# Attention with a gated feed-forward layer: projections as a stream of row-tile pairs, one-chunk score visits, AV of two head pairs a visit

## The chip, the cores and the metric

The kernel runs on one core of a Trainium2 chip. A span that the profile gives is a little shorter than the time (466.3 us beside 468.95 for the kernel before); spans are compared with spans and times with times.

## The reference

```
scores = q @ k.T / sqrt(64)                 # 8 batches, 12 heads, 448 positions, head size 64
attn   = max(scores, 0)**2 / 448
x      = (attn @ v), heads side by side     # 3584 x 768
xn     = x / sqrt(mean(x*x) + 1e-6) * rms_g
out    = (silu(xn @ w_gate) * (xn @ w_val)) @ w_out    # 768 -> 1536 -> 768
```

## The kernel before

Everything is bf16 into fp32 sums. Batch 0's attention runs first. Then, for each batch, the feed-forward layer of batch b (24 projections of 6 matmul steps, then 3 or 4 row blocks of the output projection of 12 steps) is the main stream on TensorE, and short visits of batch b+1's attention are woven into it, so that ScalarE and VectorE can work on relus and squares meanwhile.

A matmul that fills the array is issued as two **column tiles**: all 128 contraction rows, 64 output columns each (128x64). The two run side by side in one bank of PSUM:

```python
def project(b, *groups):                          # one or more of the 24 projections
    pss = [ps_m.tile([P, S], FP32, name="psP", tag="mm") for _ in groups]
    for kt in range(KT):
        for ps, (w_sb, fb) in zip(pss, groups):
            for h in range(0, P, D):              # two column halves
                nc.tensor.matmul(
                    out=ps[h : h + D, :], lhsT=w_sb[:, kt, fb * P + h : fb * P + h + D],
                    rhs=xns[b][:, kt, :], start=(kt == 0), stop=(kt == KT - 1))
```

The scores contract over 64 only, so they are **row tiles** (64x128): head 0 on rows 0 to 63, head 1 on rows 64 to 127, in two banks. A visit computes two chunks of keys; every second visit is followed by AV of the head pair before:

```python
for j in range(HP):                               # 6 head pairs
    add(0.5, lambda j=j: scores(b, j, (0, 1)))    # two chunks a visit
    ...
    add(1.2, lambda j=j: scores(b, j, (2, 3)), lambda j=j: j and attend(b, j - 1))
```

PSUM has eight banks: two score buffers of two banks (`ps_s`), one for AV (`ps_a`), and three single banks (`ps_m`) for everything else. Gates (`psP<-xn,wg_sb`) are read by a silu on ScalarE, values (`psP<-xn,wv_sb`) by the product `hT` on VectorE, outputs (`psO`) by a copy on ScalarE. Relus are on ScalarE for three chunks of four and on VectorE for the fourth; squares are on VectorE.

Of the kernel before, what the change touches and what calls it, by code (L numbers as in the profile page):

```python
# [15 lines left out]


def merge(main, side, head=0.0, tail=0.0):


    total = sum(c for c, _ in main)
    if not main:
        return [f for _, f in side]
    out, done, k = [], 0.0, 0
    n = len(side)
    for c, f in main:
        while k < n and done >= total * (head + (1.0 - head - tail) * k / n):
            out.append(side[k][1])
            k += 1
        out.append(f)  # L30
        done += c
    out.extend(f for _, f in side[k:])
    return out
# [3 lines left out]
def kernel(  # L37
# [30 lines left out]
    apool = ctx.enter_context(tc.tile_pool(name="attn", bufs=10))  # L68
# [6 lines left out]
    ps_a = ctx.enter_context(tc.tile_pool(name="ps_a", bufs=1, space=bass.MemoryType.PSUM))  # L75
    ps_m = ctx.enter_context(tc.tile_pool(name="ps_m", bufs=3, space=bass.MemoryType.PSUM))
# [117 lines left out]
    def scores(b, j, cs):  # L194

        pss = []
        for c in cs:
            psS = ps_s.tile([P, 2, 512], FP32, name="psS", tag="psS")
            for hh in range(2):
                prt = slice(hh * D, (hh + 1) * D)  # L200
                nc.tensor.matmul(  # L201
                    out=psS[:, hh, :S],
                    lhsT=qkT[b][prt, j].rearrange("p t s -> p (t s)")[:, c * PC : c * PC + P],
                    rhs=qkT[b][prt, j, 1, :],
                    start=True,
                    stop=True,
                )
            pss.append(psS)
        squares = []
        for c, psS in zip(cs, pss):  # L210
            r = apool.tile([PC, 2, S], BF16, name="r", tag="r")
            if relu_on(b, j, c) == "dve":
                nc.vector.tensor_relu(out=r[:], in_=psS[:PC, :, :S])  # L213
            else:
                nc.scalar.activation(out=r[:], in_=psS[:PC, :, :S], func=ACT.Relu)  # L215
            eng = nc.gpsimd if square_on(b, j, c) == "pool" else nc.vector
            squares.append(
                lambda r=r, eng=eng: eng.tensor_tensor(out=r[:], in0=r[:], in1=r[:], op=ALU.mult)  # L218
            )
            rsq[b, j, c] = r  # L220
        flush()
        pending.extend(squares)
# [3 lines left out]
    def attend(b, j):  # L226
        psAV = ps_a.tile([P, S], FP32, name="psAV", tag="ps_a")
        for c in range(NCH):
            for hh in range(2):
                nc.tensor.matmul(  # L230
                    out=psAV[hh * D : (hh + 1) * D, :],
                    lhsT=ld["v", b][:, 2 * j + hh, c * D : (c + 1) * D],
                    rhs=rsq[b, j, c][:, hh, :],
                    start=(c == 0),
                    stop=(c == NCH - 1),
                )
        if j == 0:
            xTs[b] = xpool.tile([P, KT, S], BF16, name="xT", tag="xT")
            x2s[b] = npool.tile([P, KT, S], BF16, name="x2", tag="x2", bufs=1)
        xT = xTs[b]  # L240
        nc.scalar.mul(out=xT[:, j, :], in_=psAV[:], mul=inv_attn)  # L241
        pending.append(
            lambda: nc.vector.tensor_tensor(  # L243
                out=x2s[b][:, j, :], in0=xT[:, j, :], in1=xT[:, j, :], op=ALU.mult
            )
        )
# [74 lines left out]
    def gate(b, fb):  # L321
        silu(b, fb, *project(b, (wg_sb, fb)))
# [100 lines left out]
```

## Time and profile before

| | before |
|---|---|
| time, median of 3 | 468.95 us (468.29 to 469.0) |
| span of the profile | 466.3 us |
| TensorE busy | 97% |
| first gate matmul begins (batch 0's attention is over) | 38.6 us |

From the page of the kernel before: the engines' busy time with its share of the span, and what the chain that ended last consists of.

```profile
PE 454.5 (97%) x4768; PEld 257.6 (55%) x4768; DVE 283.6 (61%) x449; ACT 252.5 (54%) x380; POOL 55.8 (12%) x48
...
PE 91%; DVE 3%; ACT 2%; DMA 1%; issue 1%; POOL 0%; ACTq 0%; DVEq 0%; POOLq 0%
```

TensorE is the limit. The chain in order of time (start, duration, what) shows how near the stream is to its best, and where it is not. One cycle in the middle, and the last batch, which has no visits:

```profile
215.97 0.48 PE psS L201 x4
216.45 2.39 PE psP L302 x24
218.84 0.48 PE psS L201 x4
219.32 0.88 PE psAV L230 x8
220.20 2.27 PE psP L302 x24
...
418.56 27.24 PE psP L302 x288
445.80 15.62 PE psO L339 x192
```

The last two lines give the rates of an undisturbed stream: 27.24 us for 144 pairs is 189 ns for a 448-wide pair, and 15.62 us for 48 pairs each of 512 and 256 columns is 325 ns for the two together. A visit of two score pairs is 0.48 us where two such pairs are 0.38, and a further part of each mode change hides in the lines after it: the whole cycle takes 6.51 us for 32 pairs, which are 6.06 us.

The waits of TensorE on other engines, in us in total, times, and the longest:

```profile
PE psS L201 <- ACT r L215: 2.6, 7, 0.4
...
PE psAV L230 <- DVE r L218: 1.0, 4, 0.5
...
PE psP L302 <- ACT sil L312: 0.3, 1, 0.3
```

The last line is a projection of batch 0 that waits for its bank, right after three that end together. No other projection and no output waits for one. A caution on reading: the profile's end of a matmul is modelled (about 0.35 us for a 448-wide one, although the next may begin after 0.19), so an "idle before" of TensorE is shorter than the time lost. The Trainium skill says of that end, too, that it is an estimate ("Perfetto Trace Analysis", Summary: the profiler window per engine type: TensorE runs to an *estimated* end). For sums I therefore use starts alone: on one half of the array, from one matmul's start to the next one's start, less the spacing of an undisturbed stream (189 ns at 448 columns; 109 at 256 and 216 at 512, which make the 325). What is left over I call a **gap**, and sort it by what the later matmul waits for in the built program. Before, gaps after 38.6 us are 21.6 us, of which 16.3 stand at changes of tiling mode.

### The profile page before, as it was taken

The numbers are of one execution on the slowest core, as the hardware profiler recorded it, in microseconds if no ns is written. First come the engines' busy times: TensorE is split into PE (matmuls) and PEld (weight loads), VectorE is DVE, ScalarE is ACT, GpSimd is POOL, SyncE is SP. The second block draws the span as 40 slices with busy tenths as digits, with TensorE's granted clock in tenths as the row PEclk, the third lists the DMA queues.
The fourth block names the chain that finished last, engine by engine and source line by source line (L and its number), as shares of the span: only waits on it lengthen the run. The fifth ranks groups of instructions, "written<-read, shape, count | busy, mean of one in ns | idle before, by whom it ended". The sixth has DMA issues, their size and how long they took to land.

```text
span 466.3 us, 10899 instructions
## 1 busy us (share of the span) xinstructions
PE 454.5 (97%) x4768; PEld 257.6 (55%) x4768; DVE 283.6 (61%) x449; ACT 252.5 (54%) x380; POOL 55.8 (12%) x48
## 2 busy tenths in 40 slices
PE   7989999999999999999999999999999999999995
PEld 3336654655456445655456554565456554577774
DVE  2876497757745677557665578457773677562210
ACT  4872476566545666546645666546665566452221
POOL 8463000421012000400004000000000000000000
PEclk9999999999999999999999999999999999999999
DMA  9999999999919920499009940086001300021013
GB/s 113 200 204 200 209 168 129 116 208 158 82 33 173 201 29 1 53 214 135 1 2 143 211 83 1 7 173 103 1 2 38 100 2 1 0 70 34 1 37 101
DMA packets 128047, 43.56 MB, mean 93 GB/s; under 512 B 100608, under 2 KB 124416, under 8 KB 128000
## 3 DMA queue, kind: packets, MB, share of 16 engines
q0 software_dynamic: 88944, 23.60, 52.0%
q1 hardware_dynamic: 39056, 19.28, 20.9%
q8 instruction: 37, 0.61, 0.5%
q14 instruction: 10, 0.08, 0.1%
HBM read 47.19 MB, written 11.01 MB: 125 GB/s over the span
## 4 chain that ended last, share of the span: by engine, by line
PE 91%; DVE 3%; ACT 2%; DMA 1%; issue 1%; POOL 0%; ACTq 0%; DVEq 0%; POOLq 0%
PE psP L302 48%; PE psO L339 23%; PE psS L201 9%; PE psAV L230 8%; DVE r L218 2%; PE psB L139 1%; PE psSS L276 1%; DMA kb<-in_k_dram 1%; ACT r L215 1%; DVE r L213 1%; PE psT L174 1%; ACT xT L241 1%; DVE x L243 0%; POOL qb L93 0%; POOL kb L93 0%
## 5 line engine op out<-in xcount | busy, mean ns | idle before, releaser
L215 ACT ACTIVATE r<-psS 112x896 bf16<-112x896 f32 x147 | 128.4, 915 | 28.6 <-PE psS L201 28.4
L302 PE MATMUL psP<-xn,wv_sb 128*64 128x448 bf16 x1152 | 126.9, 353 | 0.3 <-ACT sil L312 0.3
L302 PE MATMUL psP<-xn,wg_sb 128*64 128x448 bf16 x1152 | 126.8, 353 | 0.0
L339 PE MATMUL psO<-wo_sb,hT 128*64 128x512 bf16 (+1 forms) x1344 | 112.5, 326 | 0.0
L317 DVE TENSOR_TENSOR hT<-sil,psP 128x448 bf16<-128x448 bf16 x96 | 59.6, 621 | 84.7 <-PE psP L302 82.6
L218 DVE TENSOR_TENSOR r<-r 112x896 bf16<-112x896 bf16 x189 | 109.9, 626 | 0.2 <-ACT r L215 0.2
L312 ACT ACTIVATE sil<-psP 128x448 bf16<-128x448 f32 x96 | 52.2, 545 | 97.2 <-PE psP L302 97.1
L339 PEld LDWEIGHTS <-hT 128*64 128x64 bf16 x1344 | 78.9, 110 | 31.7 <-issue 0.4
L302 PEld LDWEIGHTS <-wg_sb 128*64 128x64 bf16 x1152 | 66.4, 110 | 45.4 <-issue 7.4
L302 PEld LDWEIGHTS <-wv_sb 128*64 128x64 bf16 x1152 | 65.5, 110 | 46.7 <-issue 10.5
L346 ACT COPY ost<-psO 128x512 f32<-128x512 f32 (+1 forms) x56 | 26.7, 478 | 73.1 <-PE psO L339 73.1
L213 DVE TENSOR_SCALAR r<-psS 112x896 bf16<-112x896 f32 x45 | 49.0, 1089 | 27.6 <-PE psS L201 27.6
L201 PE MATMUL psS<-qkT 64*128 64x448 bf16 x384 | 54.0, 354 | 3.3 <-ACT r L215 2.6
L230 PE MATMUL psAV<-r,vb 112*64 112x448 bf16 x384 | 46.1, 358 | 1.0 <-DVE r L218 1.0
L285 DVE RECIPROCAL rstd<-rstd 128x448 f32<-128x448 f32 x8 | 23.6, 2953 | 19.9 <-ACT rstd L281 19.9
L201 PEld LDWEIGHTS <-qkT 64*128 64x128 bf16 x384 | 11.9, 94 | 37.7 <-issue 33.1
L230 PEld LDWEIGHTS <-vb 112*64 112x64 bf16 x384 | 18.4, 109 | 24.0 <-issue 15.3
L243 DVE TENSOR_TENSOR x<-xT 128x448 bf16<-128x448 bf16 x48 | 18.5, 385 | 20.7 <-ACT xT L241 20.7
L241 ACT ACTIVATE xT<-psAV 128x448 bf16<-128x448 f32 x48 | 26.2, 545 | 8.2 <-PE psAV L230 6.6
L93 POOL DMA_DIRECT2D vb<-in_v_dram x9 | 8.7, 970 | 178.7 <-PE psAV L230 177.5
L288 DVE SCALAR_TENSOR_TENSOR xn<-xT,g_sb,rstd 128x448 bf16<-128x448 bf16 x48 | 29.3, 680 | 0.3
L95 POOL DMA_DIRECT2D qb<-in_q_dram x6 | 13.8, 2299 | 43.7 <-DMA qkT<-qb 38.1
(29 smaller groups left out, 126.3 us busy)
## 6 DMA issues: line engine op xcount, KB each, us to landing
qb<-in_q_dram POOLq DMA_DIRECT2D x7, 672.0 KB, 13.4
kb<-in_k_dram POOLq DMA_DIRECT2D x7, 672.0 KB, 19.9
vb<-in_v_dram POOLq DMA_DIRECT2D x7, 672.0 KB, 8.2
out_dram<-ost SPq DMA_DIRECT2D x8, 336.0 KB, 3.7
wg_sb<-in_moe_w_gate_dram POOLq DMA_DIRECT2D x4, 576.0 KB, 18.0
wv_sb<-in_moe_w_val_dram POOLq DMA_DIRECT2D x4, 576.0 KB, 19.7
wo_sb<-in_moe_w_out_dram POOLq DMA_DIRECT2D x2, 1152.0 KB, 26.2
out_dram<-ost SPq DMA_DIRECT2D x8, 288.0 KB, 4.6
```

Source lines behind the costliest of these rows:

```text
L201: nc.tensor.matmul(out=psS[:, hh, :S], lhsT=qkT[b][prt, j].rearrange("p t s -> p (t s)")[:, c * PC : c * PC + P], rhs=qkT[b][prt, j, 1, :] ...
L213: nc.vector.tensor_relu(out=r[:], in_=psS[:PC, :, :S])
L215: nc.scalar.activation(out=r[:], in_=psS[:PC, :, :S], func=ACT.Relu)
L218: lambda r=r, eng=eng: eng.tensor_tensor(out=r[:], in0=r[:], in1=r[:], op=ALU.mult)
L230: nc.tensor.matmul(out=psAV[hh * D : (hh + 1) * D, :], lhsT=ld["v", b][:, 2 * j + hh, c * D : (c + 1) * D], rhs=rsq[b, j, c][:, hh, :], st ...
L241: nc.scalar.mul(out=xT[:, j, :], in_=psAV[:], mul=inv_attn)
L288: nc.vector.scalar_tensor_tensor(out=xn[:, kt, :], in0=xTs[b][:, kt, :], scalar=g_sb[:, kt : kt + 1], in1=rstd[:], op0=ALU.mult, op1=ALU.mult,
L302: nc.tensor.matmul(out=ps[h : h + D, :], lhsT=w_sb[:, kt, fb * P + h : fb * P + h + D], rhs=xns[b][:, kt, :], start=(kt == 0), stop=(kt == ...
L312: nc.scalar.activation(out=s[:], in_=psG[:], func=ACT.Silu)
L317: nc.vector.tensor_tensor(out=hTs[b // 2][:, fb, o : o + S], in0=sil[b, fb][:], in1=psV[:], op=ALU.mult)
L339: nc.tensor.matmul(out=ps[h : h + D, :w], lhsT=hTs[i][:, fk, t * P + h : t * P + h + D], rhs=wo_sb[:, fk, o : o + w], start=(fk == 0), sto ...
L346: nc.scalar.copy(out=ost[:, o : o + w], in_=ps[:, :w])
```

## The change

The intent: let the projections run in the same tiling mode as the scores, so that a score visit changes no mode. Each projection is cut along its contraction instead of its output columns: row tiles 64x128, an upper half (rows 0 to 63) and a lower half, which add into the same bank. Two row tiles must not write one bank at once (the Trainium skill, "TensorEngine Tiling (Array Packing)", Gotcha 1), so the upper half of one group (the *leader*) runs beside the lower half of an earlier one (the *follower*). One matmul of each makes a *slot*, and the number of slots by which the lower half of a group comes after its upper half is the *trail*. Outputs become three pieces of 256 in place of 512 and 256. Score visits take one chunk, AV takes two head pairs into a score buffer, and the freed bank makes `ps_m` four.

```diff
-    ps_a = ctx.enter_context(tc.tile_pool(name="ps_a", bufs=1, space=bass.MemoryType.PSUM))
-    ps_m = ctx.enter_context(tc.tile_pool(name="ps_m", bufs=3, space=bass.MemoryType.PSUM))
+    ps_m = ctx.enter_context(tc.tile_pool(name="ps_m", bufs=4, space=bass.MemoryType.PSUM))
...
+            for c in range(NCH):
+                if c == 1 and j in (2, 4):
+                    add(1.6, lambda j=j: attend(b, j - 2))          # AV of two pairs
+                add(0.3, lambda j=j, c=c: scores(b, j, c))          # one chunk
...
+    class Stream:
+        APART = 2
+        def pick(self, half, taken):
+            here = self.at[half]
+            order = ([here] if here in self.open else []) + self.open
+            for g in order:
+                if g is not taken and g.ready(half):
+                    return g
+            if half == 0 and self.todo:
+                g = self.todo.pop(0); self.open.append(g); g.begin()   # takes a bank
+                return g
+        def step(self):                                             # one slot: leader and follower
+            lead = self.pick(0, None)
+            follow = self.pick(1, lead)
+            ...
+    class Group:
+        def ready(self, half):
+            if self.last not in (None, half) and self.rest < stream.APART:
+                return False
+            return self.count[half] < (self.count[0] if half else self.bound())
+        def emit(self, half):
+            if self.last not in (None, half):
+                tc.add_manual_dep(nc.tensor.nop().ins, self.mm.name, behind)
+            mm = nc.tensor.matmul(out=self.ps[:, : self.w], lhsT=self.lhsT(i)[prt], rhs=self.rhs(i)[prt], ...)
+    class Piece(Group):                                             # an output piece, one of a trio
+        def bound(self):
+            h = self.n // 2
+            if self.count[0] >= h and any(g.count[0] < h for g in self.trio):
+                return h
+            return self.n
```

(The code is shortened, and lines are drawn together. Cut: the norm's sums become a group of the stream; `xn` has one buffer instead of two and `attn` twelve instead of ten; the weaving counts slots of the leader.)

More of the change, by code (lines that the diff above doesn't have):

```diff
@@ L15 @@
 NCH = 4
-def merge(main, side, head=0.0, tail=0.0):
-    total = sum(c for c, _ in main)
-    if not main:
-        return [f for _, f in side]
-    out, done, k = [], 0.0, 0
-    n = len(side)
-    for c, f in main:
-        while k < n and done >= total * (head + (1.0 - head - tail) * k / n):
-            out.append(side[k][1])
-            k += 1
-        out.append(f)
-        done += c
-    out.extend(f for _, f in side[k:])
-    return out
 @with_exitstack
@@ L67 @@
     qtpool = ctx.enter_context(tc.tile_pool(name="qkT", bufs=2))
-    apool = ctx.enter_context(tc.tile_pool(name="attn", bufs=10))
+    apool = ctx.enter_context(tc.tile_pool(name="attn", bufs=12))
     xpool = ctx.enter_context(tc.tile_pool(name="xT", bufs=1))
@@ L192, in flush, with scores @@
             pending.pop(0)()
-    def scores(b, j, cs):
-        pss = []
-        for c in cs:
-            psS = ps_s.tile([P, 2, 512], FP32, name="psS", tag="psS")
-            for hh in range(2):
-                prt = slice(hh * D, (hh + 1) * D)
-                nc.tensor.matmul(
-                    out=psS[:, hh, :S],
-                    lhsT=qkT[b][prt, j].rearrange("p t s -> p (t s)")[:, c * PC : c * PC + P],
-                    rhs=qkT[b][prt, j, 1, :],
-                    start=True,
-                    stop=True,
-                )
-            pss.append(psS)
-        squares = []
-        for c, psS in zip(cs, pss):
-            r = apool.tile([PC, 2, S], BF16, name="r", tag="r")
-            if relu_on(b, j, c) == "dve":
-                nc.vector.tensor_relu(out=r[:], in_=psS[:PC, :, :S])
-            else:
-                nc.scalar.activation(out=r[:], in_=psS[:PC, :, :S], func=ACT.Relu)
-            eng = nc.gpsimd if square_on(b, j, c) == "pool" else nc.vector
-            squares.append(
-                lambda r=r, eng=eng: eng.tensor_tensor(out=r[:], in0=r[:], in1=r[:], op=ALU.mult)
-            )
-            rsq[b, j, c] = r
+    def scores(b, j, c):
+        psS = ps_s.tile([P, 2, 512], FP32, name="psS", tag="psS")
+        for hh in range(2):
+            prt = slice(hh * D, (hh + 1) * D)
+            nc.tensor.matmul(
+                out=psS[:, hh, :S],
+                lhsT=qkT[b][prt, j].rearrange("p t s -> p (t s)")[:, c * PC : c * PC + P],
+                rhs=qkT[b][prt, j, 1, :],
+                start=True,
+                stop=True,
+            )
+        r = apool.tile([PC, 2, S], BF16, name="r", tag="r")
+        if relu_on(b, j, c) == "dve":
+            nc.vector.tensor_relu(out=r[:], in_=psS[:PC, :, :S])
+        else:
+            nc.scalar.activation(out=r[:], in_=psS[:PC, :, :S], func=ACT.Relu)
+        eng = nc.gpsimd if square_on(b, j, c) == "pool" else nc.vector
@@ L221, in scores @@
         flush()
-        pending.extend(squares)
+        pending.append(lambda: eng.tensor_tensor(out=r[:], in0=r[:], in1=r[:], op=ALU.mult))
+        rsq[b, j, c] = r
     x2s = {}
     def attend(b, j):
-        psAV = ps_a.tile([P, S], FP32, name="psAV", tag="ps_a")
-        for c in range(NCH):
-            for hh in range(2):
-                nc.tensor.matmul(
-                    out=psAV[hh * D : (hh + 1) * D, :],
-                    lhsT=ld["v", b][:, 2 * j + hh, c * D : (c + 1) * D],
-                    rhs=rsq[b, j, c][:, hh, :],
-                    start=(c == 0),
-                    stop=(c == NCH - 1),
-                )
+        psAV = ps_s.tile([P, 2, 512], FP32, name="psAV", tag="psS")
@@ L237, in attend @@
+        for jj in range(2):
+            for c in range(NCH):
+                for hh in range(2):
+                    nc.tensor.matmul(
+                        out=psAV[hh * D : (hh + 1) * D, jj, :S],
+                        lhsT=ld["v", b][:, 2 * (j + jj) + hh, c * D : (c + 1) * D],
+                        rhs=rsq[b, j + jj, c][:, hh, :],
+                        start=(c == 0),
+                        stop=(c == NCH - 1),
+                    )
         if j == 0:
@@ L239, in attend @@
             x2s[b] = npool.tile([P, KT, S], BF16, name="x2", tag="x2", bufs=1)
-        xT = xTs[b]
-        nc.scalar.mul(out=xT[:, j, :], in_=psAV[:], mul=inv_attn)
+        xT = xTs[b][:, j : j + 2, :]
+        nc.scalar.mul(out=xT, in_=psAV[:, :, :S], mul=inv_attn)
         pending.append(
-            lambda: nc.vector.tensor_tensor(
-                out=x2s[b][:, j, :], in0=xT[:, j, :], in1=xT[:, j, :], op=ALU.mult
-            )
+            lambda: nc.vector.tensor_tensor(out=x2s[b][:, j : j + 2, :], in0=xT, in1=xT, op=ALU.mult)
         )
@@ L256, in attention @@
         for j in range(HP):
-            add(0.5, lambda j=j: scores(b, j, (0, 1)))
-            if b < PE_T and j + 1 < HP:
-                add(0.4, lambda j=j: transposes(b, j + 1))
-            if b == 0:
-                add(0.3, lambda: keep_busy(2))
-            add(1.2, lambda j=j: scores(b, j, (2, 3)), lambda j=j: j and attend(b, j - 1))
-            if b == 0:
-                add(0.3, lambda: keep_busy(2))
+            for c in range(NCH):
+                if c == 1 and j in (2, 4):
+                    add(1.6, lambda j=j: attend(b, j - 2))
+                add(0.3, lambda j=j, c=c: scores(b, j, c))
+                if c == 1 and b < PE_T and j + 1 < HP:
+                    add(0.4, lambda j=j: transposes(b, j + 1))
+                if b == 0 and c % 2:
+                    add(0.3, lambda: keep_busy(2))
@@ L265, in attention, with __init__, add, first @@
         add(0.1, flush)
-        add(0.8, lambda: attend(b, HP - 1), flush)
+        add(1.6, lambda: attend(b, HP - 2), flush)
         return units
     xns, hTs = {}, {}
+    class Stream:
+        APART = 2
+        def __init__(self):
+            self.todo, self.open, self.at = [], [], [None, None]
+        def add(self, groups):
+            self.todo += groups
+        def first(self, groups):
+            self.todo[:0] = groups
+        def pick(self, half, taken):
[5 more added lines that the diff above has]
+            if half == 0 and self.todo:
+                g = self.todo.pop(0)
+                self.open.append(g)
+                g.begin()
+                return g
+            return None
+        def step(self):
+            if not (self.todo or self.open):
+                return False
+            lead = self.pick(0, None)
+            follow = self.pick(1, lead)
+            for half, g in ((0, lead), (1, follow)):
+                if g is not None:
+                    g.emit(half)
+            self.at = [lead, follow]
+            for g in self.open:
+                g.rest += 1
+            if follow is not None and follow.count[1] == follow.n:
+                self.open.remove(follow)
+                follow.done(follow.ps)
+            return True
+        def run(self):
+            while self.step():
+                pass
@@ new lines, with __init__, begin @@
+    stream = Stream()
+    behind = mybir.DependencyInfo(mybir.DependencyClass.Sync, mybir.DependencyReason.DATA)
+    class Group:
+        handed = 0
+        def __init__(self, n, w, lhsT, rhs, done, name):
+            self.n, self.w, self.lhsT, self.rhs, self.done, self.name = n, w, lhsT, rhs, done, name
+            self.count, self.rest, self.last = [0, 0], 0, None
+        def bound(self):
+            return self.n
+        def ready(self, half):
+            if self.last not in (None, half) and self.rest < stream.APART:
+                return False
+            return self.count[half] < (self.count[0] if half else self.bound())
+        def begin(self):
+            self.ps = ps_m.tile([P, 512], FP32, name=self.name, tag="mm")
+        def emit(self, half):
+            i = self.count[half]
+            prt = slice(half * D, (half + 1) * D)
+            if self.last not in (None, half):
+                tc.add_manual_dep(nc.tensor.nop().ins, self.mm.name, behind)
+            mm = nc.tensor.matmul(
+                out=self.ps[:, : self.w], lhsT=self.lhsT(i)[prt], rhs=self.rhs(i)[prt],
+                start=(half == 0 and i == 0), stop=(half == 1 and i == self.n - 1),
+            )
+            self.count[half] += 1
+            self.last, self.rest = half, 0
+            self.mm = mm.ins
@@ new lines, with __init__, bound, norm_sums @@
+    class Piece(Group):
+        def __init__(self, trio, *args):
+            super().__init__(*args)
+            self.trio = trio
+            trio.append(self)
+        def bound(self):
+            h = self.n // 2
+            if self.count[0] >= h and any(g.count[0] < h for g in self.trio):
+                return h
+            return self.n
+    def norm_sums(b):
+        return Group(
+            KT, S, lambda i: ones_bf[:], lambda i: x2s[b][:, i, :],
+            lambda ps: norm_scale(b, ps), "psSS",
+        )
@@ L272, in norm @@
     def norm(b):
-        psSS = ps_m.tile([P, S], FP32, name="psSS", tag="mm")
+        psSS = ps_m.tile([P, 512], FP32, name="psSS", tag="mm")
         for kt in range(KT):
@@ L276, in norm, with norm_scale @@
                 nc.tensor.matmul(
-                    out=psSS[h : h + D, :], lhsT=ones_bf[:, h : h + D], rhs=x2s[b][:, kt, :],
+                    out=psSS[h : h + D, :S], lhsT=ones_bf[:, h : h + D], rhs=x2s[b][:, kt, :],
                     start=(kt == 0), stop=(kt == KT - 1),
                 )
+        norm_scale(b, psSS)
+    def norm_scale(b, psSS):
         rstd = npool.tile([P, S], FP32, name="rstd", tag="rstd", bufs=1)
         nc.scalar.activation(
-            out=rstd[:], in_=psSS[:], func=ACT.Sqrt, scale=1.0 / float(DM), bias=eps_col[:]
+            out=rstd[:], in_=psSS[:, :S], func=ACT.Sqrt, scale=1.0 / float(DM), bias=eps_col[:]
         )
@@ L285, in norm @@
         nc.vector.reciprocal(out=rstd[:], in_=rstd[:])
-        xn = npool.tile([P, KT, S], BF16, name="xn", tag="xn")
+        xn = npool.tile([P, KT, S], BF16, name="xn", tag="xn", bufs=1)
         for kt in range(KT):
@@ L319, in hidden, with projection @@
         )
-    def gate(b, fb):
-        silu(b, fb, *project(b, (wg_sb, fb)))
-    def value(b, fb):
-        hidden(b, fb, *project(b, (wv_sb, fb)))
+    def projection(b, w_sb, fb, then):
+        return Group(
+            KT, S, lambda i: w_sb[:, i, fb * P : (fb + 1) * P], lambda i: xns[b][:, i, :],
+            lambda ps: then(b, fb, ps[:, :S]), "psP",
+        )
     def gate_value_gate(b):
@@ L333, with outproj, store @@
     osts = {}
-    def outproj(i, t, o, w):
-        ps = ps_m.tile([P, 512], FP32, name="psO", tag="mm")
-        for fk in range(FT):
-            for h in range(0, P, D):
-                nc.tensor.matmul(
-                    out=ps[h : h + D, :w], lhsT=hTs[i][:, fk, t * P + h : t * P + h + D],
-                    rhs=wo_sb[:, fk, o : o + w], start=(fk == 0), stop=(fk == FT - 1),
-                )
-        if o == 0:
-            osts[i, t] = opool.tile([P, DM], FP32, name="ost", tag="ost")
-        ost = osts[i, t]
+    OW = DM // 3
+    def outproj(i, t):
+        trio = []
+        for o in range(0, DM, OW):
+            Piece(
+                trio, FT, OW, lambda fk: hTs[i][:, fk, t * P : (t + 1) * P],
+                lambda fk, o=o: wo_sb[:, fk, o : o + OW],
+                lambda ps, o=o: store(i, t, o, OW, ps), "psO",
+            )
+        return trio
+    def store(i, t, o, w, ps):
+        if (i, t) not in osts:
+            osts[i, t] = [opool.tile([P, DM], FP32, name="ost", tag="ost"), 0]
+        ost = osts[i, t][0]
         nc.scalar.copy(out=ost[:, o : o + w], in_=ps[:, :w])
-        if o + w == DM:
+        osts[i, t][1] += w
+        if osts[i, t][1] == DM:
             g, end = t * P, (t + 1) * P
@@ L358, in ffn @@
     def ffn(b):
-        units = []
-        if b == 0:
-            units.append((3.4, lambda: gate_value_gate(b)))
+        groups = []
         for fb in range(FT):
             if b or fb > 1:
-                units.append((1.13, lambda fb=fb: gate(b, fb)))
+                groups.append(projection(b, wg_sb, fb, silu))
             if b or fb:
-                units.append((1.13, lambda fb=fb: value(b, fb)))
+                groups.append(projection(b, wv_sb, fb, hidden))
         full = S // P
         for t in range(full) if b % 2 == 0 else range(full, NT):
-            units.append((2.56, lambda t=t: outproj(b // 2, t, 0, 512)))
-            units.append((1.28, lambda t=t: outproj(b // 2, t, 512, DM - 512)))
-        return units
+            groups += outproj(b // 2, t)
+        return groups
     keep_busy(16)
-    for fn in merge([], attention(0) + [(1.1, lambda: norm(0))]):
+    for _, fn in attention(0) + [(1.1, lambda: norm(0))]:
         fn()
@@ L383 @@
         if b + 1 < B:
-            side = attention(b + 1) + [(1.1, lambda b=b: norm(b + 1))]
-        main = ffn(b)
+            side = attention(b + 1) + [(0.0, lambda b=b: stream.first([norm_sums(b + 1)]))]
+        if b == 0:
+            gate_value_gate(b)
+        groups = ffn(b)
+        slots = sum(g.n for g in groups)
+        stream.add(groups)
+        head, tail = 0.25 if b == 0 else 0.0, 0.18
         if b + 2 < B:
@@ L388 @@
                 load(nm, b + 2)
-            at = len(main) * 2 // 3
-            main[at:at] = [(0, lambda b=b: transpose_dma(b + 2))]
-        for fn in merge(main, side, 0.3 if b == 0 else 0.0, 0.18):
+            side.insert(len(side) * 2 // 3, (0, lambda b=b: transpose_dma(b + 2)))
+        cost = {KT: S / 2.4 + 2.5, FT: OW / 2.4 + 2.5}
+        total = sum(g.n * cost[g.n] for g in groups)
+        done, k = 0.0, 0
+        for g in groups:
+            for _ in range(g.n):
+                while k < len(side) and done >= total * (head + (1 - head - tail) * k / len(side)):
+                    side[k][1]()
+                    k += 1
+                stream.step()
+                done += cost[g.n]
+        for _, fn in side[k:]:
             fn()
+    stream.run()
 _INS = ['q', 'k', 'v', 'moe_w_gate', 'moe_w_val', 'moe_w_out', 'moe_rms_g']
```

## The prediction

> **What bounds the kernel now.** TensorE: 97% busy on the page, 91% of the chain of waits; the waits view shows it waiting under 5 us. The stream runs at line rate: in the chain, the last batch's 288 half-matmuls of the projections take 27.24 us, 189 ns per pair of column halves. From 38.6 us (first gate matmul) to about 461.4, pairs at such rates make about 403 us (projections 218, output 109, scores 32, AV 32, norm sums 8, transposes 4). 20 us are left. The timeline of 215.9 to 222.4 shows where: a cycle of 24 projection pairs, two score visits and one AV is 32 pairs = 6.06 us, but takes 6.51. So 0.45 us per cycle goes at four changes between 128x64 (or 112x64) and 64x128 tiles, 0.11 us each; 42 cycles are 19 us. The Trainium skill, "TensorEngine Tiling (Array Packing)", Key Properties, says that a change of tiling mode drains TensorE; the trace agrees (weight loads idle 0.37 us at each change).
>
> **What the change does.** Projections become 64x128 row tiles, the scores' own mode. Left are AV (3 visits a batch, 6 changes, 0.7 us against 2.7) and batch 1's transposes (12 new changes, 1.4 us in all). Gain: about 14 us less 1.4.
>
> **What it costs** (slots counted from the diff; estimates from the durations above):
> - Halves of unlike width. In the first trio of output pieces the follower finds nothing for 6 slots, so it then trails by 13 slots for good. At each change from projection to output some 13 leading 256-wide slots (109 ns) run beside 448-wide ones (189 ns); the norm-sum slots do the same. About 140 such slots x 80 ns = 11 us, plus 13 slots alone at the end, 1.4 us. This takes matmuls to start in order, as "TensorE: Matmul & The Clock Gate", Part 3, says; no run here shows it yet.
> - 256+256+256 for 512+256: 1 us.
> - PSUM. Trailing by 13, three of four banks are open when a group begins; the free one ended only six slots earlier: 1.13 us in the projections, 0.65 us in the output (before: 2.4 us). Evacuation takes about 0.35 us of matmul latency + 0.545 (silu) or 0.621 (hidden product), 1.0 us, if ACT or DVE is free at once. A relu is 0.915 on ACT, 1.089 on DVE, a square 0.626, and DVE is some 70% busy there. So PE will newly wait, perhaps 0.1 us per group: 10 to 20 us.
> - About 390 PE no-ops at half changes, 80 with a wait only two or six slots old: 1 to 4 us.
> - Start: AV of the last two pairs comes later: 1 us.
>
> ACT loses 48 copies of 0.545 us for 24 of about 0.92, off the path.
>
> **Sum.** Before the stalls a wash; with them slower. I temper that, because stalls delay the relus that cause them: **476 us, 454 to 500**. Faster by over 2%: 0.20; within 2%: 0.32; slower: 0.48.
>
> **Signs.** Right: no gaps at score visits (about 0.2 us per visit); waits of psP/psO matmuls on silu, hidden product and copy totalling 8 to 25 us; slots of 189 ns where output leads projection; output steps of about 110 ns. Wrong: those waits near zero, or mixed slots at their mean.
>
> **What would make it wrong.** Row tiles drifting apart freely (mixed slots cost nothing, about 460); evacuation mostly in time (about 466); 128-column weight loads for both halves not fitting a 109 ns slot, or the no-ops emptying PE's queue (over 500).

## More of the kernel before

The metric is the device time of one execution in microseconds, as a median of runs.

A no-op that waits for the group's last matmul is put in wherever a group changes halves; in the built program it becomes a wait of the weight load.

## The result, and the profile after

| | before | after |
|---|---|---|
| time, median | 468.73 us (468.29 to 469.0, 4 runs) | 488.44 us (488.23 to 489.29, 4 runs) |
| ratio | | 1.0422 (95% interval 1.04 to 1.0443) |
| span of the profile | 466.3 us | 486.5 us |
| first gate matmul begins | 38.6 us | 40.5 us |
| gaps on the leading half after that | 21.6 us | 37.4 us |
| ... at mode changes | 16.3 us | 6.6 us |
| ... a group begins and waits for its bank | 0.4 us | 26.8 us |
| follower alone at the end | 0 | 1.5 us |

The page of the changed kernel, the same lines:

```profile
PE 463.5 (95%) x5440; PEld 294.1 (60%) x5440; DVE 283.7 (58%) x425; ACT 256.9 (53%) x384; POOL 55.8 (11%) x48
...
PE 83%; DVE 9%; ACT 5%; issue 2%; DVEq 0%
```

TensorE's share of the chain fell from 91% to 83%, and VectorE's rose from 3% to 9%. The chain in order of time, a stretch with score visits, and the last batch:

```profile
215.06 0.19 PE psS L179 x2
215.25 1.14 PE psP L317 x12
216.39 0.19 PE psS L179 x2
216.58 1.14 PE psP L317 x12
...
223.43 0.21 PE psS L179 x2
223.66 0.78 DVE r L188
224.44 0.23 issue
224.66 0.61 DVE r L193
225.28 0.54 DVE hT L393
...
225.86 0.74 PE psP L317 x6
...
436.21 26.20 PE psP L317 x269
464.87 16.63 PE psO L317 x273
```

The first four lines are the intent fulfilled: a score visit of one pair costs 0.19 us, exactly its own matmuls. The next ones are new: the chain leaves TensorE and goes through VectorE, which does a relu, a square and then the product `hT`, which alone would free the bank that the projection at 225.86 us needs. (That TensorE isn't named there doesn't mean that it stood still for 2.2 us: the timeline has its projections and a score visit going on until the leader's matmul of 225.15. The next could have begun at 225.34 and began at 225.86, so 0.52 us are lost.) The last batch has no visits: its projections still run at line rate, but its outputs take 16.63 us where they took 15.62.

The waits of TensorE, after:

```profile
PE psP L317 <- DVE hT L393: 7.1, 14, 1.0
...
PE psO L317 <- ACT ost L427: 3.3, 6, 0.6
...
PE psS L179 <- ACT r L190: 2.6, 8, 0.4
```

The three lines shown add up to 13.0 us, 10.4 of them waits of the stream for a bank, where the gaps by starts at such places are 26.8: that is the caution above, in numbers.

One such wait close up, from the timeline of the changed kernel (start, duration, engine, what, and in brackets idle time and its releaser); weight loads are left out:

```profile
239.90 1.09 DVE L188 TENSOR_SCALAR r<-psS 112x896 bf16<-112x896 f32 x1 [1.04 <-PE psS L179]
...
240.91 0.61 DVE L193 TENSOR_TENSOR r<-r 112x896 bf16<-112x896 bf16 x1
...
241.11 0.37 PE L317 MATMUL psP<-xn,wg_sb 64*128 64x448 bf16 x2
...
241.44 0.61 DVE L393 TENSOR_TENSOR hT<-sil,psP 128x448 bf16<-128x448 bf16 x1
...
242.11 0.35 PE L317 MATMUL psP<-xn,wv_sb 64*128 64x448 bf16 x1 [0.63 <-DVE hT L393]
```

The value group's follower began its last matmul at 239.99 us, so its sum was there at about 240.34. VectorE was in a relu of 1.09 us and then in a square, began the product at 241.44 and ended it at 242.05. The leader's last matmul began at 241.11 and the next could have begun at 241.30; it began at 242.11. The bracket says 0.63 us, the gap by starts is 0.81.

Why did this not happen before? In the program one can count how many slots pass between the last matmul of the group that held a bank and the first of the group that takes it. Before it was 13 pairs, some 2.4 us. After, it is six slots for 161 of 189 projections and 64 of 84 output pieces: 1.13 us and 0.65 us, because the follower trails the leader by 13 slots and so three banks of four are held when a group begins.

### The profile page after: what moved, and what is told of

The parts are those of the page before. It is cut to its first block, busy times and chain, and to the rows that moved or that the text cites. A ratio compares the mean times of both kernels' runs of the same rounds, so it can differ in the third digit from the quotient of the medians.

```text
span 486.5 us, 12218 instructions
## 1 busy us (share of the span) xinstructions
PE 463.5 (95%) x5440; PEld 294.1 (60%) x5440; DVE 283.7 (58%) x425; ACT 256.9 (53%) x384; POOL 55.8 (11%) x48
## 4 chain that ended last, share of the span: by engine, by line
PE 83%; DVE 9%; ACT 5%; issue 2%; DVEq 0%
PE psP L317 41%; PE psO L317 21%; PE psAV L203 8%; PE psS L179 7%; DVE r L188 3%; DVE r L193 3%; ACT r L190 2%; PE psSS L317 2%; PE psB L120 2%; DVE hT L393 2%; PE psT L155 1%; ACT xT L214 1%; DVE xn L364 1%; PE psP L378 1%; DVE rstd L361 1%
## 5 line engine op out<-in xcount | busy, mean ns | idle before, releaser
L317 PE MATMUL psP<-xn,wv_sb 64*128 64x448 bf16 x1140 | 173.6, 349 | 7.1 <-DVE hT L393 7.1
L317 PE MATMUL psP<-xn,wg_sb 64*128 64x448 bf16 x1128 | 175.3, 350 | 0.5 <-ACT sil L388 0.4
L317 PE MATMUL psO<-wo_sb,hT 64*128 64x256 bf16 x2016 | 150.6, 269 | 3.3 <-ACT ost L427 3.3
L317 PEld LDWEIGHTS <-hT 64*128 64x128 bf16 x2016 | 116.4, 94 | 24.5 <-issue 10.6
L317 PEld LDWEIGHTS <-wg_sb 64*128 64x128 bf16 x1128 | 74.4, 94 | 56.4 <-issue 15.0
L317 PEld LDWEIGHTS <-wv_sb 64*128 64x128 bf16 x1140 | 75.0, 94 | 47.9 <-issue 5.0
L179 PE MATMUL psS<-qkT 64*128 64x448 bf16 x384 | 77.9, 350 | 3.6 <-ACT r L190 2.6
L427 ACT COPY ost<-psO 128x256 f32<-128x256 f32 x84 | 31.1, 371 | 45.5 <-PE psO L317 40.6
L214 ACT ACTIVATE xT<-psAV 128x896 bf16<-128x896 f32 x24 | 22.0, 917 | 45.6 <-PE psAV L203 40.1
L216 DVE TENSOR_TENSOR x<-xT 128x896 bf16<-128x896 bf16 x24 | 15.0, 623 | 30.3 <-ACT xT L214 30.3
## 6 DMA issues: line engine op xcount, KB each, us to landing
wg_sb<-in_moe_w_gate_dram POOLq DMA_DIRECT2D x4, 576.0 KB, 19.3
```

What stands on the lines that cost most here:

```text
L179: nc.tensor.matmul(out=psS[:, hh, :S], lhsT=qkT[b][prt, j].rearrange("p t s -> p (t s)")[:, c * PC : c * PC + P], rhs=qkT[b][prt, j, 1, :] ...
L214: nc.scalar.mul(out=xT, in_=psAV[:, :, :S], mul=inv_attn)
L317: mm = nc.tensor.matmul(out=self.ps[:, : self.w], lhsT=self.lhsT(i)[prt], rhs=self.rhs(i)[prt], start=(half == 0 and i == 0), stop=(half = ...
L427: nc.scalar.copy(out=ost[:, o : o + w], in_=ps[:, :w])
```

## The experiments

Theory A: TensorE waits because a bank is needed too soon after its group ended, and that is so because the follower trails by 13 slots. Rival B: the cost is in TensorE's own queue (no-ops, weight loads behind them, more visits). Rival C: one-chunk visits load ScalarE and VectorE too much or too unevenly, whatever the distance.

### The trail cut to 7 slots

```diff
-            if self.count[0] >= h and any(g.count[0] < h for g in self.trio):
+            mates = self.trio[: self.trio.index(self)]
+            if self.count[0] >= h and (
+                any(g.count[0] < h for g in self.trio) or any(g.count[0] < self.n for g in mates)
+            ):
                 return h
```

> One line of the stream's bookkeeping: a piece may begin its second half only when the earlier pieces of its trio have finished theirs. Counted in the program: the follower then trails by 7 slots throughout instead of 13, two groups are open when one begins instead of three, and a bank was given up 12 slots before it is used again instead of 6. Same matmuls, same evacuations, same visits, same number of no-ops (each of which now stands only two slots behind the matmul it waits for). Theory A (bank reuse too soon, because of the trail): PE's waits for the hidden product, silu and output copy, about 27 us on the leading half of the changed kernel, fall under 6 us; total 461 to 467 us, faster than before. Rival B (the cost sits in PE's own order: no-ops, weight loads behind them, more visits): no better than the changed kernel, or worse, 486 to 500. Rival C (ScalarE and VectorE are simply too loaded by one-chunk visits, whatever the bank distance): 480 to 488.

Measured: 469.23 us (468.83 to 470.63), ratio to before 1.0026 (1.001 to 1.0043). Bank waits fell from 26.8 to 1.1 us, and gaps from 37.4 to 18.7. In the list of TensorE's waits neither `psP` nor `psO` occurs any more; its longest lines are:

```profile
PE psS L179 <- ACT r L190: 3.0, 9, 0.4
PE psB L120 <- DVE eps_col L127: 1.3, 1, 1.3
```

A stands: one condition of bookkeeping, with the same matmuls and evacuations, gives back 19 us. (The expectation has one thing wrong: in the program the half changes, each with its no-op, rise from 392 to 448, and most of them stand two slots behind their matmul. By B this kernel should be the slower one.) B and C predicted no better than 480. But the time missed A's range by 2 us. Two things were left: the start (first gate matmul at 40.9 us) and 5.4 us of gaps before output matmuls that wait for nothing themselves. These show something else. From the timeline of this run, TensorE's matmuls alone; here the leader has output pieces (`psO`, 256 wide) and the follower the norm's sums (`psSS`, 448 wide):

```profile
248.75 0.36 PE L317 MATMUL psSS<-x,ones_bf 64*128 64x448 bf16 x1
248.76 0.39 PE L317 MATMUL psO<-wo_sb,hT 64*128 64x256 bf16 x2
248.95 0.35 PE L317 MATMUL psSS<-x,ones_bf 64*128 64x448 bf16 x1
248.99 0.38 PE L317 MATMUL psO<-wo_sb,hT 64*128 64x256 bf16 x2
249.14 0.35 PE L317 MATMUL psSS<-x,ones_bf 64*128 64x448 bf16 x1
249.21 0.38 PE L317 MATMUL psO<-wo_sb,hT 64*128 64x256 bf16 x2
249.33 0.73 PE L317 MATMUL psSS<-x,ones_bf 64*128 64x448 bf16 x3
249.75 1.64 PE L317 MATMUL psO<-wo_sb,hT 64*128 64x256 bf16 x24
```

In the program they alternate, one and one. On the chip six `psO` begin at steps of 109 ns (248.76 to 249.31) while four `psSS` begin at steps of 189: the halves do not keep step. Then the leader stops from 249.31 to 249.75, behind a weight load of the follower that waits for a matmul of the other half, and loses another 147 ns at the next such place. 329 and 147 ns over the usual spacing are 476, and six slots times the difference of 80 ns are 480. So here the difference in width is paid after all, at the next waits that tie the halves. Later runs show that this isn't a fixed price: at the same six slots 262 ns are lost with the ties three slots old, and 277 with four.

### The visits alone

Before's projections in column tiles, with one-chunk score visits, AV of two pairs, and four single banks.

```diff
 # the kernel before, plus of the change only:
-            add(0.5, lambda j=j: scores(b, j, (0, 1)))
-            add(1.2, lambda j=j: scores(b, j, (2, 3)), lambda j=j: j and attend(b, j - 1))
+            for c in range(NCH):
+                if c == 1 and j in (2, 4):
+                    add(1.6, lambda j=j: attend(b, j - 2))
+                add(0.3, lambda j=j, c=c: scores(b, j, c))
```

> The other half of the change alone: before's column-tile projections and outputs, with one-chunk score visits, AV of two pairs a visit, and four single banks. Each visit now pays two changes of tiling mode of about 0.1 us; 24 score visits and 3 AV visits a batch make some 51 changes instead of 24. Theory A: about +17 us of mode changes and nearly no waits for evacuation, as the reuse distance in column tiles is 18 pairs: 482 to 490 us. Rival C (visits overload ScalarE and VectorE): over 495, with waits of the projections on silu and hidden product over 10 us.

Measured: 491.69 us (491.65 to 493.79), ratio 1.0515 (1.0491 to 1.0539). Gaps at mode changes doubled, 16.3 to 32.5 us. The chain of this run:

```profile
216.91 0.30 PE psS L197 x2
217.21 1.25 PE psP L290 x12
```

The same visit that costs 0.19 us in a row-tile stream costs 0.30 here, and the twelve matmuls after it 1.25 instead of 1.14. The prediction of +17 us was of the right size for the mode changes (+16.2). The total missed A's range by 1.7 us: the first gate matmul was 1.9 us later as well, and 5 us of other gaps came up, for the greater part where AV waits for squares and where score visits and projections wait for relus and the norm. The list of waits has no projection waiting for silu or product. C falls: the visits alone don't make evacuation late where a bank comes back after some 19 pairs. The stream of row tiles is what makes one-chunk visits affordable.

### Relus all on ScalarE

The changed kernel, batches 1 to 7.

```diff
-        return "dve" if c == 3 and (b or j % 2) else "act"
+        return "dve" if b == 0 and c == 3 and j % 2 else "act"
```

> The changed kernel with every relu of batches 1 to 7 on ScalarE (42 relus of 1.09 us leave VectorE, 42 of 0.92 us come to ScalarE). Theory A in its finer form (the hidden product comes late behind a relu and a square on VectorE): the projections' waits on the hidden product, about 10 us on the leading half, fall under 4; waits on silu rise from under 2 to 3 to 8; the output pieces' waits on the copy stay near 10 or rise. Total 480 to 487 us. If VectorE's queue were not the cause, the waits on the hidden product would stay near 10 and the total would rise over 489.

Measured: 481.30 us (480.94 to 482.49), ratio 1.0283 (1.0268 to 1.0298). Projections' waits that end with the product fell from about 10 to 1.3 us, those that end with silu rose from 1.7 to 3.1, and output pieces that wait for a copy stayed at 10.4. All as expected. The long relu and the square behind it on VectorE decide how late a value's bank is given up, and with them gone the projections' bank waits fell from 11.6 to 4.4 us and the total by 7.

### Six single banks, one score buffer

```diff
-    ps_s = ...(tc.tile_pool(name="ps_s", bufs=2, ...
-    ps_m = ...(tc.tile_pool(name="ps_m", bufs=4, ...
+    ps_s = ...(tc.tile_pool(name="ps_s", bufs=1, ...
+    ps_m = ...(tc.tile_pool(name="ps_m", bufs=6, ...
```

> The changed kernel, trail of 13 slots kept, with one score buffer of two banks instead of two buffers, and six single banks instead of four: the bank that a group takes was given up at least 18 slots before. Theory A: waits of psP and psO on evacuation vanish (under 3 us in all), and new waits of the score visits on the relu of the visit before appear (one buffer: a visit needs the last relu done, about 1.4 us after the last visit began, and visits come every 1.2 to 1.4 us), 10 to 40 us. Total 470 to 495 us; the waits by tile are the test, not the total. Rival B or C: waits of psP or psO stay over 15 us.

Measured: 529.93 us (527.6 to 530.12), ratio 1.1306 (1.1281 to 1.133). The test by tile came out for A: bank waits 0.5 us with the 13-slot trail untouched, and the waits moved to the score visits (36.7 us of gaps):

```profile
PE psS L179 <- ACT r L190: 20.4, 37, 1.0
PE psS L179 <- DVE r L188: 7.1, 18, 0.6
PE psS L179 <- ACT xT L214: 2.6, 4, 1.0
```

The total missed its range by 35 us, for the most part as I had not thought of batch 0, where no stream hides the wait for the one score buffer: the first gate matmul began at 66.1 us instead of 40.5. The stalls of the score visits also give evacuation more time, so this run alone would not prove A; the 7-slot trail has no such stalls.

### Four slots apart, on the 7-slot trail

```diff
-        APART = 2
+        APART = 4
```

> The trail-7 kernel with a group's other half allowed four slots after its last matmul instead of two: the trail is 9 slots, a bank is free 10 slots before it is used again, and each weight load that waits for the matmul of the other half waits for one four slots old. In the trail-7 kernel 5.4 us of the leading half's gaps stood at output matmuls with no wait of their own, behind such a weight load in PE's queue. If those are the cost of the no-ops: they fall under 2.5 us, bank waits stay under 3 us, total 464 to 467.5 us, 2 to 5 us under the trail-7 kernel. If the gaps have another cause (weight loads that do not fit an output slot): total within 1 us of the trail-7 kernel's 469.2.

Measured: 468.28 us (467.82 to 468.5), ratio 0.9991 (0.9974 to 1.0007). The range was missed. Gaps between output matmuls without a bank wait fell only from 5.4 to 4.6 us, and bank waits rose from 1.1 to 4.0 with the distance cut from 12 slots to 10. So a no-op's being young is not the whole of it. At the norm's sums it does count: with the same six slots of unlike width the loss fell from 476 to 277 ns. But the longer trail brought new gaps, where each batch's outputs begin. The widths make the drift, the ties decide how much of it is paid and when; no run separates the two.

### AV of one pair in batch 0; and in every batch

Both vary the run with four slots apart.

```diff
-                if c == 1 and j in (2, 4):
-                    add(1.6, lambda j=j: attend(b, j - 2))
+                if not (b == 0) and c == 1 and j in (2, 4):      # second run: never
+                    add(1.6, lambda j=j: attend(b, j - 2))
                 add(0.3, lambda j=j, c=c: scores(b, j, c))
+                if (b == 0) and c == 3 and j:                    # second run: always
+                    add(0.8, lambda j=j: attend(b, j - 1, 1))
...
```

> The same, with AV of one pair a visit in batch 0 alone, where no stream runs beside it. In the changed kernel the first gate matmul began at 40.5 us, before at 38.6; the last AV began its last pair 1.1 us later, and the last copy and square are twice as wide. If that is the cost of AV of two pairs: the first gate matmul begins at 38.6 to 39.6 us, total 1 to 2 us under the run with four slots apart. If one-chunk visits are the cause, no change.

Measured: 468.44 us (467.81 to 471.99), ratio 1.0013 (0.9975 to 1.0051). No change, and the first gate matmul stayed at 41.1 us: AV of two pairs is not what delays the start. The expectation names one-chunk visits as the other cause, but in batch 0 this run has the matmuls of the kernel before in the same order, so that isn't shown either. A caution: each start is read from one profile, and profiles with the same batch 0 differ (40.5 to 41.1 us in five, and 41.1 and 40.2 in this run and the next).

> The same with AV of one pair a visit in every batch: six AV visits a batch instead of three, so 42 more mode changes of about 0.1 us in batches 1 to 7 against the run with batch 0 alone. If AV of two pairs is worth its mode changes: 4 to 5 us slower than that run, mode changes on the leading half 10 to 12 us instead of 6 to 7. If it is worth nothing: within 1 us.

Measured: 471.39 us (471.0 to 472.43), ratio 1.0064 (1.0049 to 1.0079). Mode changes rose from 7.1 to 11.6 us, as expected for 42 more; the total rose by only 3, because bank waits fell from 4.0 to 1.8 and the start of the profiled run was 0.9 us earlier, which is scatter, as batch 0 is the same. AV of two pairs earns its place.

### Score visits of two chunks in the row-tile stream

This varies the run with four slots apart, too.

```diff
-            for c in range(NCH):
-                if c == 1 and j in (2, 4):
+            for c in (0, 2):
+                if c == 2 and j in (2, 4):
...
-                add(0.3, lambda j=j, c=c: scores(b, j, c))
+                add(0.6, lambda j=j, c=c: scores(b, j, c), lambda j=j, c=c: scores(b, j, c + 1))
```

> The run with four slots apart, with score visits of two chunks again (both chunks' matmuls in one visit, AV of two pairs kept). In row tiles a score visit changes no mode, so 12 visits or 24 should cost the same: within 1.5 us of that run. If one-chunk visits matter for how evenly ScalarE and VectorE are fed, bank waits rise from under 3 us to over 6 us and the total by 3 us or more.

Measured: 489.18 us (488.5 to 489.94), ratio 1.044 (1.0425 to 1.0456). A clear miss: 21 us slower than with one-chunk visits. Mode changes were equal (6.7 us), but a visit now needs both score buffers at once, which it shares with AV: 13.2 us of gaps stand at score matmuls. Bank waits of the stream rose only from 4.0 to 4.7. The other loss is in output matmuls that wait for the product itself:

```profile
PE psO L317 <- DVE hT L396: 6.6, 3, 5.9
```

Most of it is a single wait of 5.9 us, which I did not explain. So one-chunk visits are needed here, but for the score buffers and not for the stream's banks.

### Batch 0 as in the kernel before; then three slots apart

On the run with four slots apart, batch 0 gets back its two-chunk visits and its AV of one pair, and AV's result goes into one of the four single banks, which are idle then, instead of into a score buffer. The second run sets `APART = 3`.

```diff
+    def attend_first(b, j):                                   # batch 0 alone
+        psAV = ps_m.tile([P, 512], FP32, name="psAV", tag="mm")
...
+        for j in range(HP if b == 0 else 0):
+            add(0.5, lambda j=j: scores_first(b, j, (0, 1)))
...
+            add(1.2, lambda j=j: scores_first(b, j, (2, 3)), lambda j=j: j and attend_first(b, j - 1))
```

> Four slots apart, trail 9, and batch 0 exactly as in the kernel before: score visits of two chunks, AV of one pair, its result in a bank of its own (one of the four single banks, idle then) instead of in one of the two score buffers. With AV of one pair in a score buffer the first gate matmul stayed at 41.1 us. If the lost 2.5 us of the start come from AV and scores sharing two buffers: the first gate matmul begins at 38.4 to 39.2 us and the total is 465 to 467 us, 0.4 to 0.9% under the kernel before. If not: 468 to 469.

Measured: 466.49 us (466.23 to 466.78), ratio 0.9959 (0.9946 to 0.9971). The first gate matmul began at 39.3 us. The range for the start was missed by 0.1 us, the total is as expected. That the start was lost by AV and scores sharing two buffers is likely, but not shown alone: against the run with AV of one pair in batch 0, TensorE's and ScalarE's work in batch 0 is in the same order, but besides AV's bank the squares stand elsewhere in VectorE's queue. Two-chunk visits with shared buffers did not help (first gate matmul at 41.8 us in the run of two chunks).

> The same with three slots apart (trail 8, a bank free 11 slots before its reuse). Bank waits should lie between those of two slots apart (about 1 us) and four (about 4 us), the gaps behind weight loads that wait for the other half between 5.4 and 4.1 us: total within 1.5 us of the run with four.

Measured: 464.34 us (464.28 to 464.51), ratio 0.9913 (0.99 to 0.9927): the best version, better than both kernels, by 0.9% over the one before (clear of the noise, though under the 2% that count as faster here). It is 2.2 us under the run before it, with four slots, where I expected 1.5 at most; 0.4 us of that is the start (38.9 us), with batch 0 the same. The last two rows of its chain show the last batch back at nearly before's rate, though the outputs are still three pieces:

```profile
414.39 26.33 PE psP L380 x276
442.05 15.73 PE psO L380 x277
```

Bank waits were 2.3 us, between 1.1 and 4.0 as expected; the unexplained output gaps were 3.5, below both 5.4 and 4.6, which I had not expected.

### The norm's sums out of the stream

```diff
-            side = attention(b + 1) + [(0.0, lambda b=b: stream.first([norm_sums(b + 1)]))]
+            side = attention(b + 1) + [(1.1, lambda b=b: norm(b + 1))]
```

> The run with three slots apart, with the norm sums of batches 1 to 7 taken out of the stream: a visit of their own in column tiles, as in the kernel before, with the same matmuls. It takes away the 448-wide slots that stand beside 256-wide ones in the output stage (6 slots x 80 ns = 0.48 us a batch, 3.4 us in seven batches, if the halves' drift is paid back at the next weight load that waits for the other half) and adds 14 mode changes of about 0.1 us, 1.4 us. If unlike widths cost what they differ by: the gaps before output matmuls with no wait of their own fall from 3.4 us to 0.5 to 1.5, total 1 to 2.5 us lower. If unlike widths cost nothing: those gaps stay, total 1 to 1.5 us higher.

Measured: 470.66 us (470.15 to 472.75), ratio 1.0055 (1.0039 to 1.0072), 6 us slower than the run it varies. Inconclusive on its question. The gaps in question fell only from 3.5 to 3.1 us, and the visit takes one of the four banks in the middle of the output stage: bank waits rose from 2.3 to 7.9 us and drowned the rest. It does show how little slack four banks leave.

### The runs side by side

Gaps in us on the leading half after the first gate matmul. "Other output" is gaps between output matmuls without a bank wait.

| run | time, us | first gate | gaps | bank | mode | score visits | other output |
|---|---|---|---|---|---|---|---|
| before | 468.73 | 38.6 | 21.6 | 0.4 | 16.3 | 0 | 0 |
| after | 488.44 | 40.5 | 37.4 | 26.8 | 6.6 | 1.3 | 1.4 |
| trail 7 | 469.23 | 40.9 | 18.7 | 1.1 | 6.9 | 1.7 | 5.4 |
| relus on ScalarE | 481.30 | 41.0 | 30.1 | 20.2 | 6.3 | 0.8 | 1.4 |
| six banks | 529.93 | 66.1 | 53.6 | 0.5 | 8.2 | 36.7 | 5.4 |
| four slots apart | 468.28 | 41.1 | 17.6 | 4.0 | 7.1 | 0.4 | 4.6 |
| three apart, batch 0 as before | 464.34 | 38.9 | 15.8 | 2.3 | 6.5 | 1.8 | 3.5 |

The trail runs and the six banks make one series: with 6, 10, 11, 12 and 18 slots between the end of a bank's group and the next one's start, bank waits are 26.8, 4.0, 2.3, 1.1 and 0.5 us.

## Why the prediction was wrong

The direction and the mechanism were right; the size was off. I put 476 us, 7 us over before, and it was 19.7 us over.

**The step that failed** is the last one: "I temper that, because stalls delay the relus that cause them: 476 us". The terms that the prediction itself lists, taken at the middle of their ranges, are -14 + 1.4 + 11 + 1.4 + 1 + 15 + 2.5 + 1 = 19.3 us. I cut 12 us off that sum with an argument that had no number; in effect the stalls, put at 10 to 20 us, were counted as 3. The runs showed bank waits of 26.8 us in their place, over even that range; the two terms that feed them (15 for PSUM, 11 for widths, see below) add to 26. Whether stalls bring any such relief was not measured; the sum without it fits. That it fits so well is partly luck: the gain at mode changes was 3 us short of its 12.6, and the two terms that make 26 can't be checked one by one.

Term by term:

- *Mode changes*, "about 14 us less 1.4": 16.3 to 6.6 us, a gain of 9.7. The mechanism was right, each change cost about 0.10 us, and score visits in the stream are free of it (1.3 us of gaps at 168 visits). The Trainium skill ("TensorEngine Tiling (Array Packing)", Key Properties: a change of mode drains TensorE) agrees with the trace. The remaining ones cost somewhat more than 0.11 us each where AV also waits.
- *PSUM*, "10 to 20 us": bank waits are 26.8 us, 11.6 of them in the projections and the rest in the outputs and norm sums. That the distance of six slots makes them, and that the trail of 13 makes the distance, is shown by the 7-slot trail (1.1 us) and by six banks with the trail kept (0.5 us). Two parts I had not costed: in the outputs even an idle ScalarE is too slow for 0.65 us (pairs of waits of 0.18 and 0.09 us in every later trio of the last batch), and around each norm ScalarE is held by two table loads of 1.28 us and a square root (one wait of 0.97 us in the stretch read closely).
- *Halves of unlike width*, "11 us": I took it that matmuls begin in program order, so that the halves keep step. They do not (my sign of 189 ns slots there failed: the leader goes on at 109). But the wide half is waited for later, so much of the difference is paid, in the changed kernel mostly as bank waits: at the last batch's change to outputs the leader lost 0.97 us, where 13 slots x 80 ns are 1.04, and 6.4 us of the 26.8 are waits of leading output pieces while the follower was still in projections, norm sums or a visit. So part of this term was counted under the wrong name, and my range for PSUM alone was not as far off as 26.8 suggests. How much of the remaining waits belongs to widths could not be separated; the run that tried to was drowned by another cost.
- *End and pieces*, 1.4 and 1 us: 1.5 and 0.8 us.
- *Start*, 1 us: 1.9 (up to 2.5 in other profiles of the same start). The reason I gave (AV of the last two pairs comes later) fell; AV in a score buffer is the likely one.
- *No-ops*, "1 to 4 us": no more than 1.4 us of output gaps could be theirs in the changed kernel.

The terms as measured: -9.7 (mode) + 26.4 (bank) - 0.9 (all other gaps) + 0.8 (pieces) + 1.9 (start) + 1.5 (end) = 20.0 us, beside 20.1 us between the spans.

## What to carry to other kernels

When a group of matmuls is spread over two passes that trail one another, count in the program how many slots lie between the end of the group that held a bank and the start of the one that takes it, and compare that time with latency + evacuation + the longest instruction that can stand in front of it. A saving on the bottleneck engine can be lost whole to that distance: here 9.7 us of mode changes were saved, 26.8 us of bank waits appeared, and one condition of ordering took nearly all of those away again. And if itemised costs add up, do not discount the sum by an argument without a number.

## What the Trainium skill lacked or had wrong

- "TensorE: Matmul & The Clock Gate", Part 3 (what overlaps and what doesn't), has matmuls in program order in start and end, strictly. Across two row tiles of unlike width the starts are not: in the 7-slot run the leader's 256-wide matmuls began every 109 ns beside 448-wide ones every 189, so that matmuls later in the program began first. The lead ended at the next two weight loads that waited for the other half, with 476 ns lost for six slots x 80 ns.
- "TensorEngine Tiling (Array Packing)", Key Properties, says that a change of mode drains TensorE but not what it costs: 0.093 to 0.104 us per change here; a one-pair score visit took 0.19 us without a change and 0.30 us with, and the twelve matmuls after it 1.14 and 1.25.
- The same list of "TensorE: Matmul & The Clock Gate", Part 3, says that a weight load overlaps running matmuls only when the row group differs (its section The mechanism also lets a load into the background weight buffer go ahead, and this trace fits that). Two streams of 64x128 row tiles with new weights in every slot ran at 189 ns per slot at 448 columns and 109 ns at 256, as the pairs of column tiles did before, although a weight load's record is 94 ns long: so each half's next load must overlap the matmul of its own rows.
- "Perfetto Trace Analysis", Identifying Performance Opportunities, says that consistent bubbles can mean too little PSUM or SBUF, which agrees with this trace; it does not say that the time from a bank's last matmul to its next first one is what to measure: 1.13 us was too short for 448 columns with relus in the queue, 0.65 us too short for 256 columns even without.
